# One core, attention and routed experts: step 5's q and k moved to SyncE in fp32, the first steps reordered, a 64 by 8 slot table

## The chip, the cores and the metric

The kernel runs on one core of a Trainium2 chip. The time is the device time of one execution, in microseconds; lower is better. Engines are named as the profile names them: PE (TensorE), DVE (VectorE), ACT (ScalarE), POOL (GpSimd), SP (SyncE).

## The reference

Attention over 8 batches and 12 heads of 448 tokens with 64 elements, with q and k normalised by their root mean square, feeds a layer of 8 experts to which a hash of the token id sends each token.

```python
q_n, k_n = rmsnorm(q, g_q), rmsnorm(k, g_k)
attn = softmax(q_n @ k_n.T / sqrt(64)); x = attn @ v          # (8, 12, 448, 64)
x = x.transpose(0, 2, 1, 3).reshape(3584, 768)
expert = token_ids * 2654435761 % 8
out[expert == e] = relu(x[expert == e] @ w1[e]) @ w2[e]        # w1 768x1024, w2 1024x768
```

All inputs are fp32, the output too. The kernel computes with fp16 and bf16 operands.

## The kernel before, in words

**Attention.** A step is a pair of heads, hp and hp + 6, of one batch; there are NS = 48 steps, six a batch. Of each step the kernel squares q and k (`prep_sq`, L365 on DVE or L363 on ACT), sums the squares by matmuls with the identity (L375) and a reduction on DVE (L390), forms the reciprocal root by Ln and Exp on ACT (L394, L400), multiplies (`prep_norm`, L423), transposes on PE (L573, or L582 to L587 for a step alone), and evacuates to qT and kT on DVE (L605, L602; kT is multiplied by g_col). Scores are four tiles a step (L613, and L616 for the last, half as wide). ACT exponentiates them, three 128x896 (L629) and one 128x448 (L632). v is copied into a wider tile (`prep_v`, L432), PE multiplies (L647, L652, L661), DVE forms reciprocals of the row sums (L670) and x (L678), and SP stores a batch's x to a scratch tensor in DRAM.

Squares, sums and roots are made by groups. Group 0 is step 0, group 1 steps 1 and 2, group 2 steps 3, 4 and 5, group 3 steps 6 and 7 (batch 1), group 4 steps 8 to 11; then a group is a batch. `ACT_SQ` lists the (group, q or k) whose squares ACT makes. v is copied by chunks: step 0, steps 1 and 2, and then three steps at a time.

**Loads.** Step 0's q and k come by SP and ACT as fp32 (`first`). All else comes by POOL, which casts to fp16 or bf16 on the way: after step 0, q and k of steps 1 and 2, v of steps 0 to 2, q and k of steps 3 and 4, batch 1's k, step 5's q and k (`load_one`), v of steps 3 to 5, batch 1's q and v, and so on. The framework gives POOL's DMAs eight semaphores in turn. An issue waits until the DMA that had its semaphore before, the eighth before it, has landed. While POOL waits, what is behind in its queue waits too. `zero` clears the parts of the tiles that a 64-partition half has no token for.

**Order.** The order of every engine's instructions is written out by hand: `emit` goes through a text of tokens. `sqk:2.0.1` is the square of k, group 2, piece 0, part 1; `sumk`, `redk`, `ln`, `er` are the further steps of a group; `nk:3`, `Tk:3`, `kT:3`, `sc:3.0`, `exp:3.0`, `av:3.0`, `rec:3`, `x:3` those of step 3; `v:2` is a chunk of v; `gain` forms g_col (L186) from the loaded g_q and g_k; `spin` issues matmuls on a cleared tile. The engines keep this order and wait by semaphores. The first text holds batches 0 and 1 and the start of batch 2, the second one (`steady`) is repeated for batches 2 to 7.

**Slot table.** Beside attention, DVE and PE work out which token sits in which slot of experts 0 and 1: `m1` to `m9` give each token a slot, `m10` to `m12` write one-hot tables of its high part (HI0 = 15 values an expert) and its low part (LO0 = 32 values), `m13a` multiplies them in 28 small matmuls (L526) for each of two tables, `m13b`, `m14` and `m15` put the four 32-partition groups together in `gidx`. `SIDE` and `AV_SIDE` say at which place of the text and at which step each one is done.

**Experts.** `hooks(s)` is called after step s - 1 and issues loads and, at step 44, three gathers of expert 0's tokens (L220), of tokens of batches 0 to 6 alone. PE transposes them at the end of attention; then each expert is two layers (L911, L928), and the rows are scattered to the output (L941).

## Time and profile before

Three runs: 355.86, 356.63, 357.22 us; median 356.63. The profiled execution took 361.06 us, with a span of 359.5 us from its first to its last instruction and a mean granted clock of 0.973.

| stage, us | PE busy | DVE busy | ACT busy | PE clock |
|---|---|---|---|---|
| 0 to 10 | 6.80 | 4.29 | 2.84 | 1.00 |
| 10 to 20 | 8.14 | 7.64 | 8.11 | 1.00 |
| 30 to 40 | 9.84 | 8.04 | 8.32 | 0.87 |
| 40 to 60 | 18.58 | 19.00 | 19.22 | 1.00 |
| 100 to 120 | 19.89 | 19.63 | 19.99 | 1.00 |
| 160 to 180 | 17.85 | 9.64 | 15.17 | 0.83 |
| 280 to 320 | 40.00 | 12.06 | 7.76 | 1.00 |

The busy time is to be held against the length of the stage. Attention lasts to some 174 us, where the first matmul of an expert starts, and the last scatter is issued at 353.9 us. In the lines of the profile a group or an instruction is written as start, duration, engine, line, operation, output<-input, shapes, count, and in brackets the idle time of its engine before it and what ended that.

### The profile page before, as it was taken

To read this page: it belongs to the slowest core of one execution; us is meant where nothing else is said; L and a number is where in the kernel's file an instruction comes from. 1 tells how busy PE (TensorE), PEld (TensorE's weight loads), DVE (VectorE), ACT (ScalarE), POOL (GpSimd) and SP (SyncE) were. 2 spreads that over 40 slices of the span, in tenths; PEclk is the share of its full clock that TensorE was granted. 3 is DMA by queue.
4 is the path that set the end of the run, shared out by engine and by line. 5 is a ranking of instruction groups with operands and counts; after the bars stand their busy time and mean duration, and the time that the engine had idled before them with its cause. 6 is when DMAs were issued, how large, how long until landed. Compare 5 with 4: busy or idle time off the path is not lost. (4 is left out here: it accounts for less than half of the span.)

```text
span 359.5 us, 9325 instructions
## 1 busy us (share of the span) xinstructions
PE 338.1 (94%) x3923; PEld 236.4 (66%) x3923; DVE 204.2 (57%) x489; ACT 190.8 (53%) x288; POOL 148.6 (41%) x210
## 2 busy tenths in 40 slices
PE   7859899999999999997999999999999999999991
PEld 3446677776777777564867866767676676766751
DVE  3866999999999999862583232332233223323210
ACT  3656999999999999997730311212211111111210
POOL 8599954332540100002374375636456461303122
PEclk9996999999999999997998999999999999999998
DMA  7999999999999999032379999999999995303012
GB/s 106 194 121 198 202 235 197 239 202 198 184 236 228 233 221 232 15 78 67 91 162 193 288 276 209 255 268 231 268 214 258 243 233 193 110 1 119 29 75 84
DMA packets 41659, 64.59 MB, mean 180 GB/s; under 512 B 9999, under 2 KB 29655, under 8 KB 41232
## 3 DMA queue, kind: packets, MB, share of 16 engines
q0 software_dynamic: 38464, 58.33, 81.3%
q1 hardware_dynamic: 2848, 5.44, 4.8%
q8 instruction: 31, 0.51, 0.5%
q10 hardware_dynamic: 304, 0.21, 0.2%
q14 instruction: 12, 0.10, 0.1%
HBM read 89.29 MB, written 17.30 MB: 296 GB/s over the span
## 5 line engine op out<-in xcount | busy, mean ns | idle before, releaser
L629 ACT ACTIVATE expT<-sc_ps 128x896 bf16<-128x896 f32 x144 | 123.4, 934 | 8.4 <-PE sc_ps L613 7.6
L928 PEld LDWEIGHTS <-h_sb 128*128 128x128 f16 (+1 forms) x512 | 51.5, 105 | 31.3 <-issue 1.3
L928 PE MATMUL o_ps<-w_sb,h_sb 128*128 128x512 f16 (+3 forms) x384 | 67.6, 330 | 0.1
L941 POOL DMA_INDIRECT out_dram<-o_sb,gidx x32 | 32.5, 1015 | 83.9 <-ACT o_sb L938 56.0
L915 ACT ACTIVATE h_sb<-h_ps 128x480 f16<-128x480 f32 (+2 forms) x44 | 21.8, 499 | 67.3 <-PE h_ps L911 58.6
L911 PEld LDWEIGHTS <-w_sb 128*128 128x128 f16 x336 | 44.2, 146 | 14.5 <-issue 0.2
L220 POOL DMA_INDIRECT kr<-x_scratch,gidx x32 | 32.5, 1015 | 46.8 <-DVE kT L602 35.0
L938 ACT COPY o_sb<-o_ps 128x768 f32<-128x768 f32 x16 | 12.8, 800 | 71.5 <-PE o_ps L928 64.3
L647 PEld LDWEIGHTS <-expT 128*128 128x128 bf16 x864 | 40.2, 99 | 14.6 <-DVE x_sb L678 8.1
L647 PE MATMUL av_ps<-v,expT 128*128 128x65 bf16 x864 | 46.8, 196 | 3.0 <-DVE x_sb L678 2.9
L911 PE MATMUL h_ps<-xT,w_sb 128*128 128x480 f16 x240 | 49.4, 366 | 0.0
L613 PE MATMUL sc_ps<-qT,kT 64*128 64x448 f16 x288 | 45.0, 364 | 1.7 <-ACT expT L629 0.6
L917 DVE TENSOR_SCALAR h_sb<-h_ps 128x480 f16<-128x480 f32 x28 | 18.4, 658 | 47.2 <-PE h_ps L911 45.4
L938 DVE COPY o_sb<-o_ps 128x768 f32<-128x768 f32 (+1 forms) x15 | 14.3, 956 | 33.6 <-PE o_ps L928 31.5
L232 DVE COPY xT<-xT_ps 128x768 f16<-128x768 f16 x28 | 15.5, 554 | 29.0 <-PE xT_ps L231 29.0
L678 DVE TENSOR_TENSOR x_sb<-av_ps,srec 128x448 f16<-128x448 f32 x48 | 29.9, 623 | 1.4
L294 POOL DMA_DIRECT2D vr<-in_v_dram x36 | 24.2, 683 | 15.0 <-DMA kr<-in_k_dram 9.2
L375 PEld LDWEIGHTS <-ident 128*128 128x128 f16 x576 | 23.2, 99 | 10.4 <-issue 6.1
L632 ACT ACTIVATE expT<-sc_ps 128x448 bf16<-128x448 f32 x48 | 27.6, 575 | 0.7 <-PE sc_ps L616 0.7
L652 PE MATMUL av_ps<-v,expT 128*128 128x130 bf16 x144 | 26.0, 225 | 0.0
L602 DVE TENSOR_SCALAR kT<-qkT_ps,g_col 128x512 f16<-128x512 f16 x48 | 21.1, 478 | 3.1 <-PE qkT_ps L573 2.2
L928 PE MATMUL o_ps<-kr,h_sb 128*128 128x512 f16 (+3 forms) x128 | 22.1, 326 | 0.0
(204 smaller groups left out, 452.9 us busy)
## 6 DMA issues: line engine op xcount, KB each, us to landing
w_sb<-in_moe_w_dram POOLq DMA_DIRECT2D x18, 512.0 KB
w_sb<-in_moe_w_dram POOLq DMA_DIRECT2D x8, 768.0 KB
kr<-in_k_dram POOLq DMA_DIRECT2D x7, 672.0 KB
qr<-in_q_dram POOLq DMA_DIRECT2D x7, 672.0 KB
x_scratch<-x_sb SPq DMA_DIRECT2D x15, 288.0 KB, 6.2
w_sb<-in_moe_w_dram POOLq DMA_DIRECT2D x2, 1536.0 KB
qr<-in_moe_w_dram POOLq DMA_DIRECT2D x6, 512.0 KB
vr<-in_v_dram POOLq DMA_DIRECT2D x14, 192.0 KB
```

The lines of the kernel that those rows point to most:

```text
L220: nc.gpsimd.indirect_dma_start(out=xg[0:idx.shape[0], :], out_offset=None, in_=x_dram[0:rows, :], in_offset=bass.IndirectOffsetOnAxis(ap=i ...
L294: eng.dma_start(out=dst[64 * half:64 * half + 64, :, s0:s0 + cnt, :].rearrange("p n s d -> p n (s d)"), in_=runs(t, h0 + HP * hh, 1, n, to ...
L613: nc.tensor.matmul(sc[:, hh, :S], lhsT=kT[64 * hh:64 * hh + 64, P * j:P * j + P], rhs=qT[64 * hh:64 * hh + 64, :], start=True, stop=True)
L629: nc.scalar.activation(expT[:, 2 * j:2 * j + 2, :], sc[:, :, :S], AF.Exp, bias=0.0, scale=1.0)
L632: nc.scalar.activation(expT[:, 6, :], sc[:, 0, :S], AF.Exp, bias=0.0, scale=1.0)
L647: nc.tensor.matmul(av[:, 2 * t + hh, :], lhsT=expT[:, tl(hh, j), P * t:P * t + P], rhs=v8[:, i, vs(hh, j), 0:D + 1], start=(hh == 0 and t ...
L652: nc.tensor.matmul(av[:, 2 * t:2 * t + 2, :], lhsT=expT[:, 6, P * t:P * t + P], rhs=v8[:, i, 0::7, 0:D + 1], start=False, stop=False)
L678: nc.vector.tensor_tensor(out=xs[b][:, :, hp * D:hp * D + D], in0=av[:, :, :D], in1=srec[:, :, None].to_broadcast([P, SL, D]), op=ALU.mult)
L911: nc.tensor.matmul(h_ps[:, :c1 - c0], lhsT=w1v[:, co, fo, :], rhs=xT[:, co, c0:c1], start=(co == 0), stop=(co == CO - 1))
L928: nc.tensor.matmul(o_ps[d0 > 0][0:w, d0:d1], lhsT=h_sb[:, fo, col * P:col * P + w], rhs=w2_sb[:, fo, d0:d1], start=(fo == 0), stop=(fo == ...
L938: (nc.vector.tensor_copy if col % 2 else nc.scalar.copy)(o_sb[0:w], o_ps[0][0:w])
L941: scat = nc.gpsimd.indirect_dma_start(out=out[:, :], out_offset=bass.IndirectOffsetOnAxis(ap=idx[0:w], axis=0), in_=o_sb[0:w], in_offset=N ...
```

## The change

- `load_one` issues step 5's q and k on SP, not POOL, right after the token ids, and so ahead of nearly all other loads. [...]the tiles are fp32, in the same buffers as before.
- On POOL batch 1's k is issued after v of steps 3 to 5.
- Group 1's k is squared on ACT and its q on DVE, where it was the other way round; group 3's k is squared on ACT too.
- The slot table has 64 low and 8 high values. One pass of 28 matmuls with 32 columns gives both tables, at step 31; before there were two passes with 30 columns, at steps 30 and 32. `m10` and `m11` are done at one place of the text.
- Expert 0's three gathers are issued at steps 44, 45 and 46, one at each.
- The first text has another order throughout. `steady` is unchanged.

```diff
-    LO0 = 32
-    HI0 = FIT // LO0
+    LO0 = 64
+    HI0 = CAP // LO0
...
             if s == 0:
                 return first[:, a]
+            if s == HP - 1:
+                return raw_at(bufs, 0, 4 * PAIR, 16 * D).bitcast(FP32).rearrange(
+                    "p (s d) -> p s d", d=D)
...
-        ACT_SQ = ((0, 1), (1, 0), (5, 0))
+        ACT_SQ = ((0, 1), (1, 1), (3, 1), (5, 0))
...
-        def m13a(av, a):
+        def m13a(av):
             for c in range(NTC):
                 g = LO0 * (c % NL)
-                nc.tensor.matmul(av[g:g + LO0, SP:SP + 2 * HI0], lhsT=lo[:, :, c],
-                                 rhs=hi[:, a, :, c], start=False, stop=(c >= NTC - NL),
+                nc.tensor.matmul(av[g:g + LO0, SP:SP + 4 * HI0], lhsT=lo[:, :, c],
+                                 rhs=hi[:, :, :, c], start=False, stop=(c >= NTC - NL),
                                  skip_group_check=True)
...
         def load_one(s):
-            load_heads([nc.gpsimd] * 4, raw(1, s)[:, None], k, s, 1)
-            load_one_q([nc.gpsimd] * 2, raw(0, s), s)
+            load_heads([nc.sync] * 4, raw(1, s)[:, None], k, s, 1)
+            load_one_q([nc.sync] * 2, raw(0, s), s)
...
         setup1()
+        load_one(HP - 1)
...
         load_pairs(q, q_bufs, 0, 3, 2 * PAIR, HP, 2)
-        load(1, "k")
-        load_one(HP - 1)
         load_v(3, 3)
-        load(1, "qv")
+        load(1)
...
-            if s == NS - 4:
-                for c in range(KT - 1):
-                    gather(xg_e[:, c], gidx[:, c:c + 1], N_EARLY)
+            if NS - 4 <= s < NS - 5 + KT:
+                c = s - NS + 4
+                gather(xg_e[:, c], gidx[:, c:c + 1], N_EARLY)
...
         emit("""
-            zero:3 zero:6 zero:0 zero:1 zero:2 sqq:0.0 sqk:0.0 spin:12 sumk:0.0 zero:7
-            redk:0.0 ln:0.1.2 spin:2 sumq:0.0 redq:0.0 er:0.1.2 ln:0.0.1 er:0.0.1
-            sqk:1.0 nk:0 spin:3 sumk:1.0 nq:0 Tk:0 gain:0 Tq:0 redk:1.0 sqq:1.0 sumq:1.0
-            kT:0 redq:1.0 ln:1 qT:0 spin:2 sc:0.0 er:1 sc:0.1 exp:0.0 sc:0.2 nk:1 nq:1
-            spin:1 Tk:1 kT:1 exp:0.1 sc:0.3 kT:2 v:0 spin:3 Tq:1 exp:0.2 v:1 qT:1 spin:1
-            sc:1.0 exp:0.3 sc:1.1 sqk:2.0.0 exp:1.0 exp:1.1 sqq:2.0.0 sc:1.2 av:0.0
-            av:0.1 qT:2 av:0.2 rec:0 sqk:2.0.1 exp:1.2 sc:1.3 sc:2.0 x:0 sqq:2.0.1
-            sumk:2.0 sc:2.1 redk:2.0 exp:1.3 sumq:2.0 exp:2.0 sc:2.2 v:2 av:1.0 av:1.1
-            redq:2.0 sqk:3.0 exp:2.1 ln:2 er:2 nk:3 exp:2.2 sc:2.3 av:1.2 exp:2.3 rec:1
-            nq:3 Tk:3 kT:3 kT:4 Tq:3 x:1 qT:3 qT:4 nk:5 av:2.0 sc:3.0 exp:3.0 nq:5
...
+            zero:1 zero:6 zero:0 gain:0 sqk:0.0 zero:2 spin:12 sumk:0.0 sqq:0.0 zero:7
+            spin:2 sumq:0.0 redk:0.0 ln:0.1.2 er:0.1.2 redq:0.0 nk:0 ln:0.0.1 zero:3
+            spin:3 Tk:0 er:0.0.1 sqk:1.0 spin:1 sumk:1.0 nq:0 sqq:1.0 Tq:0 redk:1.0 kT:0
+            sumq:1.0 redq:1.0 qT:0 ln:1 v:1 spin:2 sc:0.0 er:1 nk:1 nq:1 sc:0.1 exp:0.0
+            spin:2 Tk:1 kT:1 sc:0.2 kT:2 v:0 sc:0.3 sqk:2.0.0 exp:0.1 exp:0.2 spin:1
+            Tq:1 qT:1 av:0.0 qT:2 sc:1.0 exp:0.3 sqk:2.0.1 sc:1.1 sc:1.2 sqq:2.0.0
+            sumk:2.0 av:0.1 sqq:2.0.1 exp:1.0 sc:1.3 exp:1.1 redk:2.0 exp:1.2 v:2
+            sumq:2.0 redq:2.0 av:0.2 sc:2.0 exp:1.3 ln:2 er:2 sc:2.1 rec:0 sc:2.2 x:0
+            exp:2.0 nk:3 av:1.0 nq:3 Tk:3 kT:3 sc:2.3 av:1.1 av:1.2 exp:2.1 kT:4 nk:5
+            Tq:3 rec:1 exp:2.2 qT:3 exp:2.3 qT:4 sc:3.0 nq:5 sc:3.1 sqk:3.0 sqq:3.0
...
```

## The prediction

> **What bounds the kernel now.** I read four views: busy time by stage, ACT's waits in two stretches, the timeline of the first 45 us, and the timeline around 161 us. The chain that ended last is no help: it holds the final scatter alone.

> Busy time by stage (length, then PE, PEld, DVE, ACT, POOL busy, clock, DMA share, GB/s):
> ```profile
> 20.00:30.00 10.00, 7.22 (x108) 5.16 (x105) 6.42 (x17) 4.63 (x9) 9.56 (x17) 0.79 1.20 154
> 60.00:80.00 20.00, 19.93 (x367) 14.10 (x365) 19.35 (x51) 20.00 (x30) 6.51 (x9) 1.00 1.34 216
> 240.00:280.00 40.00, 40.00 (x252) 27.63 (x251) 12.62 (x19) 6.97 (x11) 21.78 (x25) 1.00 1.04 246
> ```
> Attention is bound by ACT from some 33 us (20.00 of 20), the experts by PE (40.00 of 40). In the first 33 us nothing is full: ACT works 4.63 us of 10. ACT's waits from 13 to 45 us (sum, count, longest):
> ```profile
> ACT expT L629 <- PE sc_ps L613: 4.7, 4, 3.1
> ACT ss L394 <- DVE ss L390: 2.7, 2, 1.8
> ACT expT L632 <- PE sc_ps L616: 0.3, 1, 0.3
> ```
> That is 7.7 us; from 45 to 165 us the same view has 1.2. So a microsecond won before step 4 passes to the end, since first ACT and then PE are full after it. The timeline shows what starves ACT:
> ```profile
> 12.74 2.54 ACT L629 ACTIVATE expT<-sc_ps 128x896 bf16<-128x896 f32 x3
> 18.44 1.82 POOL L294 DMA_DIRECT2D vr<-in_v_dram x3 [3.34 <-DMA kr<-in_k_dram]
> 22.59 0.56 DVE L432 COPY v<-vr 128x1536 bf16<-128x1536 bf16 x1 [2.05 <-DMA vr<-in_v_dram]
> 23.34 0.33 ACT L394 ACTIVATE ss<-ss,eps_col 128x44 f32<-128x44 f32 x1 [1.84 <-DVE ss L390]
> 24.70 0.62 PE L573 MATMUL qkT_ps<-ident,n_k 128*128 128x128 f16 x8 [1.76 <-DVE n_k L423]
> 26.00:27.00 1.00, 0.71 (x7) 0.71 (x8) 0.77 (x2) 0.00 (x0) 0.95 (x2) 0.50 1.28 183
> 28.30 2.54 ACT L629 ACTIVATE expT<-sc_ps 128x896 bf16<-128x896 f32 x3 [3.07 <-PE sc_ps L613]
> 33.50 2.53 ACT L629 ACTIVATE expT<-sc_ps 128x896 bf16<-128x896 f32 x3 [0.51 <-PE sc_ps L613]
> ```
> Read downwards: POOL cannot issue three of the four loads of v for steps 3 to 5 until batch 1's k has landed (18.4), so v lands at 22.5. DVE stands before its copy, with redq:2, nk:3 and nq:3 behind it. PE idles, its clock goes to 0.50 (until 32.6), and step 3's scores come at 28.30. Step 4 begins at 33.50. The sum closes: 12.74 + four steps of 2.54 + 0.42 (11.84) + ln and er of groups 2 and 3 (4 x 0.3 = 1.2) + 7.7 idle = 33.5.

> [...] little work from 22.9 to 25.7, then 0.50 for 6.8 us. [...] The trace of before does not show such a contest of large loads. So I count step 5's loads as moved in the stream, not removed.

> **The change part by part.**

> *Step 5 by SyncE.* Six issues leave POOL (0.54 x 4 + 0.64 + 0.61 = 3.4 us) and go on SP behind tid, where only stores follow, from 45 us on. With batch 1's k put behind them, v's four loads now wait for the landings of k and q of steps 1-2 and of two pieces of the first v, by the eight semaphores that POOL's DMAs take in turn. The landing events of before: k of steps 1-2 at 8.80, q 10.07, v 11.89, k of 3-4 13.10, q 14.21, batch 1's k 18.16, step 5 19.42. Step 5 took 1.26 of the stream; ahead of it, it delays the others by 0 to 1.27 us (q's own 10.07 - 8.80). I take the late end: k 10.1, q 11.3, v 13.2, k and q of 3-4 14.4 and 15.5, v of 3-5 1.82 later (as v of 0-2 took), 17.3, batch 1's k 21.3 (3.95), q 25.2 (before 28.3). The 0.94 us wait for step 5's k at 18.98 goes as well. fp32 costs DVE 0.69 for 0.43 on two squares and 0.65 for 0.42 on two norms: about 1.0 us.

> *Order, the start.* g_col now stands ahead of the first q square, and waits for gcol, which landed at 6.86: square 7.3 (before 6.44), k's er 9.0, nk:0 9.0-9.65, three memsets 0.3, nq:0 to 10.65. The q square of group 1 waits on DVE for q (11.3), with redk, kT:0, redq and qT:0 queued behind, and PE's first scores behind these: 11.95, 12.15, 12.6, 12.85, 13.2; an exponential 0.4 later (as 12.34 to 12.74): 13.7. With q at 10.07 it is 12.9. So this part loses 0.2 to 1.0.

> *Order, steps 1 to 3.* With full durations in DVE's queue: v:1 and nk:1, nq:1 end 14.9, kT twice 15.8, v:0, one square, qT:1 at 17.2: step 1's exponential 17.6 (ACT idle 1.0). Then three more squares 19.5, redk 19.7, v:2 (landed 17.3) 20.3, redq 20.8, ln and er 21.4, step 2 at 21.4 (idle 0.2). rec, x, nk:3, nq:3 end 23.0, kT twice 23.9, Tq:3 24.5, qT:3 25.1: step 3 at 25.5, while ACT squares batch 1's k (landed 21.3) from 24.4 to 25.35 (idle 0.2). That square, 0.95, is the one added to ACT; group 1's only changes from q to k. Its DVE price was 0.62. q's square at 26.0 finds q landed.
> Step 4 then starts at 13.7 + 11.84 + 1.2 + 0.95 + 1.4 idle = 29.1, against 33.5: **4.4 us earlier**. Unknown are the first exponential (12.9 to 13.7) and the idle (0.6 to 3.4, where 3.4 gives every one of some 35 DVE instructions 0.06 more); the ends are 27.5 and 31.1, a gain of 6.0 to 2.4.

> *Slot table.* 28 matmuls (0.65 us by the row of L526: 1.3 for 56) go from PE. DVE, before: 2 x 0.37 + 2 x 0.35 + 2 x 0.38 + 2 x 0.19 + 4 x 0.16 = 3.2; after, by half and double size: 4 x 0.2 + 2 x 0.7 + 0.4 + 0.3 = 2.9. Hidden by ACT, which has 19.99 and 19.13 of 20 there. POOL's setup is about as long (one iota shorter, one longer) and hidden by 5 us of slack or more. Cost 0, bounds -0.5 to +0.3.

> *Gathers.* By the instruction lists of the two built programs nothing lies between the three gathers on POOL in either, and their waits are the same kinds: the program's later place adds no wait. The first one waits for batch 6's stores (landed 160.0), not for steps 44 to 46. Cost 0.

> **To the end.** Batch 2's and 3's loads land 3 us earlier; the nearest use in before was v of batch 2, 4.4 us after landing (42.1 to 46.5), and v:5 now stands a step later, so no wait returns. The experts' weights landed by 144.6, used from 174. Thus 359.5 - 4.4 = 355.1 in this execution. Its run took 361.06, 4.43 above the median of 356.63, so it holds some chance delay; from the median: 356.63 - 4.4 = **352.2**.

> **The rivals.**
> 1. *The stop at 164 us belongs to the gathers and goes.* Around it:
> ```profile
> 163.86 1.00 POOL L220 DMA_INDIRECT kr<-x_scratch,gidx  x1 [0.30 <-issue]
> 164.00:165.00 1.00, 0.30 (x2) 0.03 (x1) 0.00 (x0) 0.00 (x0) 0.86 (x1) 1.00 0.64 164
> 165.46 0.21 DVE L670 RECIPROCAL srec<-av_ps 128x7 f32<-128x7 f32 x1 [2.34 <-PE sc_ps L613]
> 165.56 2.54 ACT L629 ACTIVATE expT<-sc_ps 128x896 bf16<-128x896 f32 x3 [1.67 <-PE sc_ps L613]
> ```
> PE, DVE and ACT stand still while POOL gathers, and the clock is 0.50 until 172.5. Eight exponentials (2 x 2.96) from 163.9 would end at 169.8, not 172.7: 2.9. For it: the place. Against it: five gathers in a row at 177 to 183 stop nobody, and the POOL queue is unchanged. 352.2 - 2.9 = 349.3.
> 2. *DVE takes the place of the loads.* In my replay its queue is never empty from 13.2 to 30. If each of 35 instructions loses 0.1, 3.5 us go: 355.7. For it: DVE is 19.35 of 20 later. Against it: its squares started 0.53 apart, not 0.62 (15.83, 16.36, 16.90).
> 3. *Slower: step 5's loads stop the first step.* The first step's own q and k, as large and fp32 by the same queues, landed from 2.86 to 6.31: 3.5 us, not 1.26. Then q of steps 1-2 lands at 13.6; DVE holds all of step 0 behind one square, PE has little from 9.7 on, and its clock halves: 29.1 + 2.3 for q + 4.0 (the waits 3.07 and 0.89 of the half-clock stage in before) = 35.4, 1.9 later than before: 358.5. [...] Against it: that early stretch held tid's tiny elements and the start of the queues.

> **How the numbers follow.** My forecast 0.70, rival 1 0.08, rival 2 0.13, rival 3 0.09. The forecast's own range is 350.6 to 354.2. The range 349.0 to 355.9 takes in rivals 1 and 2 and leaves rival 3 and a little more out. A measurement here tells about 0.5% (1.8 us) from no change, so faster is below 354.8: 0.78; same 0.13; slower 0.09.

> **What would show it.** Right: no DVE wait for vr near 22; no POOL wait for kr ahead of vr; clock 1.00 from 20 to 33; step 4's first exponential near 29; ACT idle under 3 us from the first exponential to 45; ACT full after. First exponential between 12.9 and 13.7, later than before. Three gathers 1.3 us apart, as now. Wrong: a first exponential past 15, a clock of 0.50 before 33, or ACT idle returning after step 4. The forecast also fails if ACT or PE of the later stages is not what passes the gain on.

## The result, and the profile after

| kernel | median us | range, runs | ratio to before, 95% interval |
|---|---|---|---|
| before | 356.45 | 355.86 to 357.22, 4 | |
| after | 351.01 | 350.48 to 351.98, 4 | 0.9849 [0.9818, 0.9880] |

The change makes the kernel 5.4 us faster; the forecast was 4.4. Executions of before spread from 353.96 to 359.37 us in the experiments below, and the two that were profiled lie at or above the slow end of that (359.25 and 361.06 us), so single stages of theirs can be longer than usual. The profiled execution of after took 351.39 us and has a span of 349.8 us. ACT's waits from 13 to 45 us (sum, count, longest) were 7.7 us; now they are:

```profile
ACT ss L395 <- DVE ss L391: 3.0, 1, 3.0
ACT expT L632 <- PE sc_ps L616: 1.3, 3, 0.8
```

The 3.0 lies ahead of the first exponential. ACT's timeline of after (start, duration, instruction, idle before it) shows the rest:

```profile
13.63 0.32 ACT L395 ACTIVATE ss<-ss,eps_col 128x28 f32<-128x28 f32 x1 [2.97 <-DVE ss L391]
...
14.62 1.73 ACT L632 ACTIVATE expT<-sc_ps 128x896 bf16<-128x896 f32 x2 [0.39 <-PE sc_ps L616]
...
18.64 2.54 ACT L632 ACTIVATE expT<-sc_ps 128x896 bf16<-128x896 f32 x3 [0.77 <-PE sc_ps L616]
...
22.09 2.51 ACT L632 ACTIVATE expT<-sc_ps 128x896 bf16<-128x896 f32 x3
...
26.01 2.54 ACT L632 ACTIVATE expT<-sc_ps 128x896 bf16<-128x896 f32 x3
...
29.34 2.54 ACT L632 ACTIVATE expT<-sc_ps 128x896 bf16<-128x896 f32 x3
```

The lines at 14.62, 18.64, 22.09, 26.01 and 29.34 open steps 0 to 4. Steps 2, 3 and 4 carry no bracket: ACT hardly idles before them (the view leaves short gaps out; the longest of these is the 0.14 us before step 3). Before, step 3 came at 28.30 after 3.07 us of idling, and step 4 at 33.50.

Busy time by stage of after (length, then PE, PEld, DVE, ACT, POOL, clock, DMA share, GB/s):

```profile
12.00:15.00 3.00, 3.00 (x31) 1.54 (x29) 2.32 (x7) 0.95 (x3) 2.59 (x5) 0.50 1.30 205
15.00:20.00 5.00, 4.41 (x59) 2.69 (x59) 4.19 (x10) 4.05 (x6) 4.52 (x7) 0.95 1.34 201
20.00:33.00 13.00, 11.75 (x220) 8.30 (x218) 12.21 (x30) 12.80 (x21) 12.17 (x30) 1.00 1.34 202
```

From 20 to 33 us ACT works 12.80 of 13.00 and the clock is 1.00. The half clock of 25.75 to 32.6 is gone, but there is one from 8.72 to 15.54. Ten of the 14 profiles of this case have one that begins in the first 13 us, before repeated among them (10.20 to 13.61); the profile from which the forecast was made has none there.

The two profiled spans differ by 9.7 us, more than the medians. The stages show why (differences of before and after): step 4's start 4.2; steps 4 to 24 0.9; step 24 to the last exponential 2.4; to the first expert matmul 0.1; the experts to PE's last matmul 1.7; the tail 0.4. Only the first is what was forecast; the experiments tell which of the others belong to the change.

### The profile page after: what moved, and what is told of

Read it like the earlier page. It is cut to its first block, busy times and chain, and to the rows that moved or that the text cites. A ratio compares the mean times of both kernels' runs of the same rounds, so it can differ in the third digit from the quotient of the medians.

```text
span 349.8 us, 9268 instructions
## 1 busy us (share of the span) xinstructions
PE 334.1 (95%) x3894; PEld 234.2 (67%) x3894; DVE 203.1 (58%) x486; ACT 190.2 (54%) x289; POOL 145.2 (42%) x202
## 5 line engine op out<-in xcount | busy, mean ns | idle before, releaser
L632 ACT ACTIVATE expT<-sc_ps 128x896 bf16<-128x896 f32 x144 | 123.7, 938 | 3.8 <-PE sc_ps L616 3.1
L928 PE MATMUL o_ps<-w_sb,h_sb 128*128 128x512 f16 (+3 forms) x384 | 66.0, 326 | 0.0
L911 PEld LDWEIGHTS <-w_sb 128*128 128x128 f16 x336 | 44.2, 146 | 14.5 <-issue 0.2
L220 POOL DMA_INDIRECT kr<-x_scratch,gidx x32 | 32.7, 1022 | 47.9 <-DVE srec L673 37.0
L650 PEld LDWEIGHTS <-expT 128*128 128x128 bf16 x864 | 38.8, 97 | 11.5 <-DVE x_sb L681 5.9
L650 PE MATMUL av_ps<-v,expT 128*128 128x65 bf16 x864 | 45.4, 193 | 1.0 <-DVE x_sb L681 1.0
L616 PE MATMUL sc_ps<-qT,kT 64*128 64x448 f16 x288 | 44.3, 358 | 1.9 <-DVE qT L608 0.7
L917 DVE TENSOR_SCALAR h_sb<-h_ps 128x480 f16<-128x480 f32 x28 | 18.4, 657 | 47.2 <-PE h_ps L911 47.2
L938 DVE COPY o_sb<-o_ps 128x768 f32<-128x768 f32 (+1 forms) x15 | 14.3, 956 | 33.7 <-PE o_ps L928 31.6
L232 DVE COPY xT<-xT_ps 128x768 f16<-128x768 f16 x28 | 15.5, 552 | 27.2 <-PE xT_ps L231 27.2
L294 POOL DMA_DIRECT2D vr<-in_v_dram x36 | 23.8, 670 | 16.1 <-DMA qr<-in_q_dram 5.7
L655 PE MATMUL av_ps<-v,expT 128*128 128x130 bf16 x144 | 25.0, 220 | 0.0
## 6 DMA issues: line engine op xcount, KB each, us to landing
qr<-in_moe_w_dram POOLq DMA_DIRECT2D x6, 512.0 KB, 13.6
vr<-in_v_dram POOLq DMA_DIRECT2D x14, 192.0 KB, 13.6
```

Of the source, the lines that this page charges most:

```text
L220: nc.gpsimd.indirect_dma_start(out=xg[0:idx.shape[0], :], out_offset=None, in_=x_dram[0:rows, :], in_offset=bass.IndirectOffsetOnAxis(ap=i ...
L294: eng.dma_start(out=dst[64 * half:64 * half + 64, :, s0:s0 + cnt, :].rearrange("p n s d -> p n (s d)"), in_=runs(t, h0 + HP * hh, 1, n, to ...
L616: nc.tensor.matmul(sc[:, hh, :S], lhsT=kT[64 * hh:64 * hh + 64, P * j:P * j + P], rhs=qT[64 * hh:64 * hh + 64, :], start=True, stop=True)
L632: nc.scalar.activation(expT[:, 2 * j:2 * j + 2, :], sc[:, :, :S], AF.Exp, bias=0.0, scale=1.0)
L650: nc.tensor.matmul(av[:, 2 * t + hh, :], lhsT=expT[:, tl(hh, j), P * t:P * t + P], rhs=v8[:, i, vs(hh, j), 0:D + 1], start=(hh == 0 and t ...
L655: nc.tensor.matmul(av[:, 2 * t:2 * t + 2, :], lhsT=expT[:, 6, P * t:P * t + P], rhs=v8[:, i, 0::7, 0:D + 1], start=False, stop=False)
```

## The experiments

All 12 were compared with before on the same chip, where it took 356.6 to 356.9 us (median of 26 to 71 runs, 353.96 to 359.37).

**1. Before once more**, with no edit.

> The kernel before, unchanged, profiled a second time. Theory (the stop of PE, DVE and ACT from 163.9 to 165.4 and the half clock from 193 were chances of one execution): no such stop near the three gathers, clock 1.00 from 160 to 200, a span near 355, step 4's first exponential again at 33.5 and the half clock again from about 25.8. Rival (the stop belongs to the gathers of before): the stop and the half clock from 165.7 return, span 359 to 360.

Measured: 357.34 us, ratio 0.9999 [0.9973, 1.0026]; step 4 at 35.11, not at 33.5 as expected. The time from step 24 to the last exponential is 72.57, not 75.34: the stop at 163 to 165 us did not recur, though the gathers are the same. So the stop does not come with the gathers, and 2.8 us of the profiled difference are chance. The half clock of the experts did recur (191.11 to 194.52; see the last section). The same kernel's step 4 differs by 1.6 us between two executions. The traces show two differences ahead of it: the loads land later in the second one (k of steps 1 and 2 at 9.88, not 8.80; v of steps 3 to 5 at 23.95, not 22.47), and its clock is 0.50 from 10.20 to 13.61. The first exponential comes at 14.45, not 12.74.

**2 to 4. The parts alone.** Loads alone: the fp32 tile and the three edits of `load_one` and the loads below. Order alone: the first text and `ACT_SQ`. Slot table and gathers alone: all the rest.

```diff
+        load_one(HP - 1)
...
-        load(1, "k")
-        load_one(HP - 1)
         load_v(3, 3)
-        load(1, "qv")
+        load(1)
```

> Before with the loads alone changed: step 5's q and k by SP in fp32, v of steps 3 to 5 ahead of batch 1's k; old order of the first steps, old slot table and gathers. Theory (v's late landing was what starved ACT): DVE no longer waits for v near 22, no half clock from 25.8, step 4 at 30.5 to 31.5, time 2 to 3 us below before. Rival (the new order carries the gain): within 0.7 us of before.

> Before with the new order of the first steps and the new list of squares on ACT alone; old loads. Theory (v's late landing starves ACT in any order): DVE waits for v until about 22.5 again, step 2's exponentials fall behind it to 24, step 4 at 31.7 to 33.7, time within 1.8 us of before. Rival (the order carries the gain): 4 us below before.

> Before with the 64 by 8 slot table in one pass and the gathers one per step alone. Theory (hidden by ACT, and the POOL queue is the same): within 0.7 us of before. Rival (the gathers' stop is real and the spread removes it, or PE's 28 fewer matmuls count): 1 to 3 us below before, and no stop near the gathers.

Measured: loads 0.9944 [0.9919, 0.9969], step 4 at 31.46; order 0.9943 [0.9918, 0.9969], step 4 at 33.59; slot table and gathers 1.0045 [1.0020, 1.0069], step 4 at 33.71. The loads and the order give 2 us each, and the third part seems to cost 1.6.

**5 and 6. After without the third part, and after without the slot table.**

```diff
-    LO0 = 64
-    HI0 = CAP // LO0
+    LO0 = 32
+    HI0 = FIT // LO0
...
-        AV_SIDE = {17: (m5a, m5b), 19: (m7a, m7b), 31: (m13a, m13b), 34: (m14a, m14b)}
+        AV_SIDE = {17: (m5a, m5b), 19: (m7a, m7b), 34: (m14a, m14b)}
+        for a in range(2):
+            AV_SIDE[30 + 2 * a] = (lambda av, a=a: m13a(av, a), lambda av, a=a: m13b(av, a))
```

> The kernel after with the old slot table (32 by 15, two passes) and the old place of the gathers: new loads and new order alone. If the parts add (loads alone 0.9944, order alone 0.9943, slot table and gathers alone 1.0045), 0.9888 or, taking the slot table's cost off the whole change, 0.9849 - 0.0045 = 0.980: about 349.5 us, faster than the kernel after by some 1.5 us, with step 4's first exponential still near 29.3 and no wait of ACT of 1.8 us at 119 to 121 us. If the prediction was right that the slot table costs nothing, the time is that of the kernel after, 0.985.

> The kernel after with the old slot table alone; the gathers stay one per step. If all the cost of the pair lies in the slot table, this equals the kernel with both undone (0.980). If the gathers' place has a part in it, it lies between that and the kernel after (0.985). Gathers predicted as no cost: they start 1.3 to 1.5 us apart in a row, at the same place, in both.

Measured: 351.64 us, 0.9879 [0.9824, 0.9934], and 351.77 us, 0.9860 [0.9814, 0.9905]. Neither beats after. So the expectation that taking the third part out gains 1.5 us failed: in the new start no cost of it in the whole time can be told from the noise. The gathers, which alone differ between the two, start some 1.44 and 1.34 us apart in a row in both. But ACT's wait of 1.8 us at 119 us is real. PE, ACT and DVE in after's timeline:

```profile
118.87 1.93 PE L527 MATMUL av_ps<-hi,lo 128*64 128x32 f16 x28
...
121.19 0.92 ACT L632 ACTIVATE expT<-sc_ps 128x896 bf16<-128x896 f32 x1 [1.77 <-PE sc_ps L616]
...
121.38 0.25 DVE L534 TENSOR_SCALAR comb<-av_ps 128x16 f16<-128x16 f32 x2 [1.76 <-PE av_ps L664]
```

and one of the two old passes, in before's timeline:

```profile
120.66 0.65 PE L526 MATMUL av_ps<-hi,lo 128*32 128x30 f16 x28
...
121.71 2.54 ACT L629 ACTIVATE expT<-sc_ps 128x896 bf16<-128x896 f32 x3 [0.59 <-PE sc_ps L613]
```

28 matmuls with 64 columns of weights take 1.93 us, and next step's scores stand behind them on PE. An old pass takes 0.65; ACT idles some 0.6 us after the first of the two and 0.1 after the second. From step 24 to the last exponential every profile with the new table takes 72.95 to 72.98 us (7 kernels), and every one with the old table 72.25 to 72.66 (6, before itself left out for its stop): the one pass costs 0.3 to 0.7 us. What offsets it in the whole time is in the last section.

The greater cost in the profile of experiment 4 lies elsewhere: between steps 4 and 8, 16.30 us against 14.97 in before repeated. (The two spans are alike all the same, 357.8 and 357.7 us, because step 4 came 1.4 us earlier in experiment 4.) Lines of POOL's and of DVE's timeline of experiment 4 stand side by side there:

```profile
42.24 2.18 POOL L181 IOTA lv<- 128x1792 int16 x1
42.61 2.22 DVE L432 COPY v<-vr 128x1536 bf16<-128x1536 bf16 x1
```

The new table's iota, the instruction on POOL that fills a tile with counting numbers, is twice as long (1.82 us against 0.97 where it runs by itself). A copy of v that takes 0.57 us in after, where it starts at 37.37 just behind the iota (35.46 to 37.28), takes 2.22 beside it. In experiments 7 and 8 the copy met the iota too and took 1.44 (steps 4 to 8: 15.5 us, against 14.5 in after, though their later loads may have a part in that). Before's own profile has such a meeting with the old, shorter iota:

```profile
41.84 1.94 DVE L432 COPY v<-vr 128x1536 bf16<-128x1536 bf16 x2
42.03 1.33 POOL L181 IOTA lv<- 128x896 int16 x1
```

The second of these two copies takes 1.37 us, and steps 4 to 8 take 15.45. So whether the two meet is a matter of timing; the new table makes a meeting longer. In the new start the copy does not come to stand behind a running iota, but it is close: in after it starts 0.09 us after the iota's end, in experiments 5, 10, 11 and 12 just before the iota's start, and there it takes 0.54 to 0.68.

**7 and 8. Which half of the loads?** In after, first batch 1's k is put ahead of v of steps 3 to 5 again; then step 5 is put back on POOL as 16 bit, with v still ahead of batch 1.

```diff
+        load(1, "k")
         load_v(3, 3)
-        load(1)
+        load(1, "qv")
```

```diff
-            load_heads([nc.sync] * 4, raw(1, s)[:, None], k, s, 1)
-            load_one_q([nc.sync] * 2, raw(0, s), s)
+            load_heads([nc.gpsimd] * 4, raw(1, s)[:, None], k, s, 1)
+            load_one_q([nc.gpsimd] * 2, raw(0, s), s)
...
-        load_one(HP - 1)
         nc.vector.memset(warm, 0.0)
...
+        load_one(HP - 1)
         load_v(3, 3)
         load(1)
```

> The kernel after with batch 1's k issued ahead of v of steps 3 to 5 again; all else as after. If v's late landing behind batch 1's k was what starved the start, v of steps 3 to 5 lands 3 to 4 us later, near 21.5 us; the copy v:2, due near 20, waits 1.2 to 1.7 us with the reductions of group 2 behind it, and step 4 begins 1.2 to 2 us later (30.5 to 31.3): 0.988 to 0.991. If the order of the instructions alone cures it, step 4 stays within 0.4 of 29.3 and the time is 0.985.

> The kernel after with step 5's q and k back on POOL as 16 bit, issued after q of steps 3 and 4; v of steps 3 to 5 and then batch 1 behind it, so of the change's loads only v ahead of batch 1's k is kept. If that order alone is what the loads are worth, v:2 does not wait for v and step 4 comes within 0.4 of the kernel after: 0.985. If taking step 5 from POOL's queue is needed (six more issues of 3.4 us ahead of v, and the wait for the eighth DMA before), v lands 2 us or more later, step 4 is 1 to 2.5 later, and the time is 0.988 to 0.992.

Measured: 355.30 us, 0.9949 [0.9924, 0.9975], step 4 at 32.58; and 356.09 us, 0.9972 [0.9945, 0.9999], step 4 at 31.43. Both undo most of the gain, more of it than expected (0.988 to 0.991 and 0.988 to 0.992). DVE's timeline of the first, then of the second:

```profile
22.59 0.91 DVE L433 COPY v<-vr 128x1536 bf16<-128x1536 bf16 x1 [2.14 <-DMA vr<-in_v_dram]
```

```profile
20.49 0.56 DVE L432 COPY v<-vr 128x1536 bf16<-128x1536 bf16 x1
...
28.56 0.63 DVE L365 TENSOR_TENSOR sq_q<-qr 128x896 f16<-128x896 f16 x1 [2.15 <-DMA qr<-in_q_dram]
```

In the first, v is late, as before the change. In the second v lands at 20.37, 2.3 us later than in after (18.06), as expected, but DVE comes to its copy no sooner than that; in after it does at 20.31. What DVE waits for is batch 1's q, which lands at 28.54 (after: 24.43). Batch 1's k is issued at 17.34 and lands 7.8 us later; in after it is issued at 13.22 and lands 7.8 us later. POOL's six issues for step 5, 3.4 us long and with waits of some 1.6 us among them, are what holds it. The stages of this kernel, then of after, show the stream running thin behind them (last column):

```profile
16.00:18.00 2.00, 1.81 (x21) 1.07 (x22) 1.82 (x5) 2.00 (x4) 2.00 (x4) 1.00 0.99 102
18.00:20.00 2.00, 1.79 (x37) 1.31 (x35) 2.00 (x6) 1.34 (x3) 2.00 (x4) 1.00 0.90 78
```

```profile
16.00:18.00 2.00, 1.81 (x24) 1.01 (x22) 1.77 (x5) 1.69 (x3) 1.93 (x4) 1.00 1.32 199
18.00:20.00 2.00, 1.60 (x29) 1.10 (x30) 2.00 (x5) 1.35 (x2) 1.96 (x3) 1.00 1.27 205
```

Not all that the second loses is lost in the start. Of the 4.9 us by which its span exceeds after's, 2.1 are there by step 4, 0.9 come between steps 4 and 8, and 1.7 are a slow clock window in the experts (last section).

**9. Before with one edit**, batch 1's k behind v:

```diff
-        load(1, "k")
         load_one(HP - 1)
         load_v(3, 3)
-        load(1, "qv")
+        load(1)
```

> The kernel before with one edit: batch 1's k issued behind step 5 and v of steps 3 to 5. If v's place behind batch 1's k was the stop of the start, DVE's wait of 2.05 us for v near 22 goes, the clock keeps 1.00 there more often, and step 4 comes 3 to 5 us earlier than the 33.5 to 35.1 of the kernel before: 0.988 to 0.994. If the old order of instructions stops the start for itself, the wait for v turns into one for batch 1's k (now later) or for the score tiles, and the time stays at 0.997 to 1.000.

Measured: 356.23 us, 0.9997 [0.9975, 1.0018]; step 4 at 34.76. The second expectation holds. DVE's timeline, and then ACT's:

```profile
21.55 0.56 DVE L432 COPY v<-vr 128x1536 bf16<-128x1536 bf16 x1
...
25.00 0.63 DVE L365 TENSOR_TENSOR sq_k<-kr 128x896 f16<-128x896 f16 x1 [2.24 <-DMA kr<-in_k_dram]
```

```profile
30.23 2.53 ACT L629 ACTIVATE expT<-sc_ps 128x896 bf16<-128x896 f32 x3 [5.44 <-PE sc_ps L613]
```

The wait for v is gone, one for batch 1's k has come in its place, and step 3's norms stand behind it in the old order.

**10 to 12. The first exponential.** It came at 14.62 where 12.9 to 13.7 was forecast. Three edits of after's first text: nine more spin matmuls; g_col formed behind `nq:0`; both, as the diff shows.

```diff
-            zero:1 zero:6 zero:0 gain:0 sqk:0.0 zero:2 spin:12 sumk:0.0 sqq:0.0 zero:7
-            spin:2 sumq:0.0 redk:0.0 ln:0.1.2 er:0.1.2 redq:0.0 nk:0 ln:0.0.1 zero:3
-            spin:3 Tk:0 er:0.0.1 sqk:1.0 spin:1 sumk:1.0 nq:0 sqq:1.0 Tq:0 redk:1.0 kT:0
+            zero:1 zero:6 zero:0 sqk:0.0 zero:2 spin:14 sumk:0.0 sqq:0.0 zero:7
+            spin:5 sumq:0.0 redk:0.0 ln:0.1.2 er:0.1.2 redq:0.0 nk:0 ln:0.0.1 zero:3
+            spin:5 Tk:0 er:0.0.1 sqk:1.0 spin:1 sumk:1.0 nq:0 gain:0 sqq:1.0 Tq:0 redk:1.0 kT:0
```

> The kernel after with nine more spin matmuls before step 0's transposes (14 for 12, 5 for 2, 5 for 3). If the late first exponential (14.62, forecast 12.9 to 13.7) is the half clock from 8.7 to 15.5 us, the clock stays 1.00 there, the first exponential comes 0.5 to 1.0 earlier and so does step 4: 0.982 to 0.984. If the wait for the gain vectors and the DVE queue set it, the first exponential stays at 14.6, or comes later by what the added matmuls hold up (up to 0.5), and the time is 0.985 or a little above.

> The kernel after with the forming of g_col moved from ahead of the first square of k to just behind the first norm of q. DVE stood 4.1 to 5.3 us before it, until the gain vectors landed (7.1 to 8.4 us). If this wait sets the first exponential (it came 7.4 us after g_col in two kernels), the first q square starts near 6.5, the first exponential 0.7 to 1.5 us earlier, and the time is 0.981 to 0.983. If the landing of q of steps 1 and 2, or the half clock, sets it, the first exponential stays within 0.3 and the time at 0.985.

> The kernel after with both edits of the start: g_col formed late, and nine more spin matmuls. If the wait for the gain vectors and the half clock each cost the first exponential about 1 us, it comes near 13.0 and step 4 near 28, the time 0.979 to 0.982, the fastest of all. If step 4 is held by the landing of v of steps 3 to 5 and by DVE's queue, the earlier first exponential turns into later waits of ACT, and the time is 0.984 to 0.986.

Measured: more spins 351.54 us, 0.9852 [0.9806, 0.9898]; late g_col 351.47, 0.9870 [0.9838, 0.9902]; both 352.44, 0.9882 [0.9848, 0.9917]. None is faster than after. With more spins the clock is 1.00 through the start, and from g_col (8.05, its load landed later here) to the first exponential 6.4 us pass, not the 7.4 of after. With g_col late the first exponential comes at 13.91, and with both at 13.94; as the clock is 1.00 there in both, what the late g_col alone gives is not separated. But step 1 stays: ACT's, then DVE's timeline with g_col late:

```profile
13.91 1.73 ACT L632 ACTIVATE expT<-sc_ps 128x896 bf16<-128x896 f32 x2
...
18.73 2.54 ACT L632 ACTIVATE expT<-sc_ps 128x896 bf16<-128x896 f32 x3 [0.73 <-PE sc_ps L616]
```

```profile
14.59 0.52 DVE L433 COPY v<-vr 128x1024 bf16<-128x1024 bf16 x1 [1.14 <-DMA vr<-in_v_dram]
```

Step 1 comes at 18.73, in after at 18.64. DVE now waits for the first v, whose copy stands ahead of step 1's norms (it landed at 14.47 in this execution, at 13.58 in after's). What step 0 wins is lost there. Moving that copy behind the norms together with g_col is the next thing to try; it was not tried.

## Why the prediction was right

**The start, and where step 4's gain comes from.** The forecast had step 4 at 29.1; it came at 29.34. The two executions of before had 33.50 and 35.11, so the gain is 4.2 to 5.8 against 4.4 (2.4 to 6.0). These signs hold: no DVE wait for v near 22, no POOL wait for k ahead of v, clock 1.00 from 20 to 33, ACT idle 1.15 us from the first exponential to step 4. Three did not come as written: the first exponential was later than 12.9 to 13.7, the clock was 0.50 before 33 (from 8.72 to 15.54), which was named as a sign of being wrong, and ACT idles 1.8 us at 119 to 121 us, after step 4. The first two belong to the term of the first exponential and the third to the slot table, both below; none of them undid the gain. That 29.1 lies so near 29.34 is in part luck: the first exponential came 0.9 us later than the sum has it, while ACT idled 0.25 less (1.15 for 1.4) and worked 0.4 less (13.58 for 13.99). The diagnosis was right but too narrow. It named v's place behind batch 1's k as what starves the start. Step 4's start over all the kernels shows that two of the three measures are not enough:

| step 5 on | first on POOL | old order | new order |
|---|---|---|---|
| POOL | batch 1's k | 33.50, 35.11 | 33.59 |
| POOL | v | 34.76 | 31.43 |
| SP | batch 1's k | not run | 32.58 |
| SP | v | 31.46 | 29.26 to 29.82 |

(The last cell is after and experiments 5 and 6; 33.71 of experiment 4 belongs to the first. Most cells are one execution, and the two of before differ by 1.6, so differences under that are not shown; that the last cell lies below all others is.) Each load is due soon after it lands. With v moved alone, the wait goes to batch 1's k in the old order and to its q in the new one. Only when six issues leave POOL's queue as well do v and batch 1 both come in time. What counts, beside the order of the landings, is the 3.4 us of issues off POOL's queue: with them on it, in experiment 8, batch 1's k is issued at 17.34 instead of 13.22, and the stream carries 102 and 78 GB/s from 16 to 20 us instead of 199 and 205.

**The landings.** Forecast and measured: k of steps 1 and 2 10.1 and 9.25, q 11.3 and 10.62, first v 13.2 and 13.58, k and q of 3 and 4 14.4 and 14.53, 15.5 and 15.64, v of 3 to 5 17.3 and 18.06, batch 1's k 21.3 and 21.03, its q 25.2 and 24.43. What the contest of SP's fp32 loads with POOL's cost can't be read from the two main profiles, because landings vary: before repeated has 9.88 and 10.99 for the first two with no edit at all. The other profiles tell more. With step 5 on POOL (five besides before's), k of steps 1 and 2 lands at 9.86 to 10.14, q at 10.97 to 11.28 and k of 3 and 4 at 13.91 to 14.18; with it on SP (seven besides after's) at 9.46 to 10.33, 11.23 to 11.65 and 15.13 to 15.60. So the first load loses nothing that can be seen, q some 0.4 us, and k of 3 and 4 some 1.4. That step 5's loads stay in the stream when SP issues them was the author's estimate; the 1.4 us, beside the 1.26 that they took in before, agree with it. The forecast's late end of 1.27 was too much for the first two and about right behind them.

**The first exponential.** The term was too small by 0.9 to 1.7 us. The replay priced PE at full clock, but the clock was 0.50 from 8.72 on. From g_col to the first exponential 7.4 us pass in after and in experiment 5, with 6.8 us of half clock, 7.15 in experiment 6, with 3.4, and 6.4 in experiment 10, with none: the half clock cost 1.0. It was not caused by q, which landed at 10.62, and old starts have it too. It cost nothing of step 4: in experiments 10 to 12 the first exponential comes at 13.91 to 14.45, but ACT then idles 1.7 to 2.2 us until step 4, not 1.15, and step 4 begins at 29.41 to 29.68.

**Slot table.** Mis-sized: its pass was priced at 0.65 us, by the row of a matmul with 32 columns of weights; it takes 1.93. Calling it hidden by ACT was wrong as well, as ACT waits for the scores behind it. The cost in attention is 0.3 to 0.7 instead of -0.5 to 0.3. POOL's setup was called hidden by slack; that holds in after, but where its longer iota met a copy of v, steps 4 to 8 took 0.9 to 1.3 us more, and the old iota met it in before's profile too.

**Gathers.** Right: no cost, and the same spacing.

**To the end.** Right that step 4's gain passes on: from step 8 to step 24 all 14 profiles take 48.40 to 48.62 us. Between steps 4 and 8, where the forecast had no gain, after takes 14.54 us and the two executions of before 15.45 and 14.97. Right also that before's profiled run held chance delay. Of the 9.7 us between the two profiles 2.8 are the stop that did not recur; 1.7 are a clock window (below). Two things can account for the distance from 352.2 to 351.01: step 4 of before came 1.6 us later in its second execution than in the one that the forecast used, and steps 4 to 8 gave 0.4 to 0.9. How often they do so, two executions don't tell.

**Rivals.** 1 fell with experiment 1. 2 fell too: DVE is busy 12.21 of 13.00 us from 20 to 33, near its limit, but ACT does not wait for it there. 3 did not occur: q landed at 10.62, not at 13.6, and the other profiles put its delay at some 0.4 us.

## What to carry to other kernels

Where several loads are each due soon after they land, moving one ahead only moves the wait to the next, as in experiments 8 and 9; write down due time against landing for the whole queue, and count the issues of the queue as well as the bytes. Price a small matmul by a row with the same number of weight columns (28 took 0.65 us with 32, 1.93 with 64), and ask which scores stand behind it on PE. A single profile of such a start is uncertain by 1 to 2 us (step 4 of before came at 33.50 and at 35.11): look at a second execution before a stop is explained.

## What was not expected of the hardware

```profile
190.82 3.33 PE L928 MATMUL o_ps<-w_sb,h_sb 128*128 128x512 f16 x8
```

```profile
185.08 1.89 PE L928 MATMUL o_ps<-w_sb,h_sb 128*128 128x512 f16 x8
```

The experts take 177.90 to 177.97 us with the slow window and 176.23 to 176.27 without. Take the time from the first expert matmul to a change of the clock, modulo 3.413: it is 0.89 to 1.65 in the seven with the slow window, and 0.14, 0.73 or 2.10 to 3.11 in the others. So the slow window goes with the phase, not with the change. The profile counts PE as busy in the whole window ahead of it in before (3.41 of 3.41 us, at clock 1.00), 2.87 us of it with these matmuls of 56 columns, and the clock went to 0.50 behind it all the same. Why was not tested. This is the 1.7 us between the two profiles, and probably part of the spread of before's runs.

**Matmuls with weights of 64 columns took three times those with 32.** 28 matmuls: 1.93 us against 0.65, or 69 ns against 23 each. Their 28 weight loads took 1.81 us in after and 0.53 in before, or 65 ns against 19 each. Why the 32-column pass takes less than half of the other was not tested; its matmuls go to four groups of columns in turn, those of 64 columns to two.

**A copy of v on DVE and the iota on POOL make each other longer.** In the four profiles in which the copy starts behind the iota it takes 1.37 to 2.22 us instead of 0.57, and it ends 0.41 to 0.42 us after the iota in each of them. Where the copy starts first it is the iota that becomes longer, as in experiment 11:

```profile
37.51 0.55 DVE L433 COPY v<-vr 128x1536 bf16<-128x1536 bf16 x1
37.57 2.21 POOL L181 IOTA lv<- 128x1792 int16 x1
```

The iota takes 2.18 to 2.21 us there and in experiments 10 and 12, not 1.82, and the old one 1.36 in experiment 5, not 0.97. Squares on DVE beside the same iota grow little or not at all: one of 128x896 takes 0.61 us in after beside it and away from it (at 35.40 and at 33.18), one of 128x1344 takes 0.85 (at 36.48 and at 45.14), and 0.93 beside it in experiments 7 and 8. So a copy that starts behind the iota becomes longer, and so does an iota that starts behind a copy; why squares hardly do was not tested.

**The tail** from PE's last matmul to the end is 6.8 to 6.9 us in all kernels with the new table, and 7.2 to 7.3 in four with the old one, but 6.8 to 7.0 in the other three with the old one. In experiments 5 and 6 it is 0.4 us longer than in after, which offsets that much of the 0.7 and 0.4 us that their old slot tables save from step 24 to the last exponential. What sets it stays open.
